# The first steps of a fused attention, ReLU-squared MLP and top-1 MoE kernel in another order

## The chip, the cores and the metric

One core of one Trainium2 chip. The metric is the device time of one execution in microseconds; lower is better.

## The reference

Inputs: q, k, v of 4 x 8 x 768 x 64, 8 memory keys and values per head, w_in 512 x 2048, w_out 2048 x 512, eight experts' w1 (512 x 1024) and w2 (1024 x 512), and two gates of 512 x 8. What is computed, cut down:

```python
for c in range(24):                      # chunks of 32 queries, 56 keys of context and 8 memory keys
    scores = scale * q_c @ concat(mem_k, k_ctx).T
    a = exp(scores - max(scores)); a /= sum(a) + 1e-9
    out[c] = a @ concat(mem_v, v_ctx)
x = out as 3072 x 512                    # tokens x (heads x 64)
r = maximum(x @ w_in, 0); x = (r * r) @ w_out
e = argmax(x @ w_gate); p = softmax(x @ w_gate)[e]; s = sigmoid((x @ w_output_gate)[e])
out = p * s * (maximum(x @ w1[e], 0) @ w2[e])
```

## The kernel before

Tokens are cut into 24 units of 128 (u), 12 pairs of units (`Duo`, d0 to d11) and, for the MLP, 12 blocks of 256 (`Block`, b0 to b11; block n is pair n). All products are 3-pass: each operand is split into a rounded part (hi) and the rest (lo), and hi x hi, lo x hi and hi x lo are added.

A pair goes through `scores_mm` (TensorE, L161), `scores_max` and `scores_sub` (VectorE, L190 and L195), `scores_exp` (ScalarE, L211), `norm` (VectorE, L217 to L221), `transpose_a_mm` and `transpose_a_copy` (TensorE L234, ScalarE L244), `av_mm` (TensorE, L161, or L259 in the later form), `av_scale` (VectorE, L274), `transpose_x_mm`, `transpose_x_hi` and `transpose_x_lo` (TensorE L234, ScalarE L299, VectorE L303). Each of these takes one unit or both.

w_in and w_out are cut into eight tiles each, i0 to i7 and o0 to o7, of 1 MB; `tiles` numbers them i0, o0, i1, o1 and so on, so number 13 is o6 and number 15 is o7. Each is loaded (`load_w`) and split in six steps: `split_w_exp` (ScalarE's Abs, L327), `split_w_shift` (VectorE, L332), `split_w_or` in two steps (VectorE, L339 and L343), `split_w_hi` (ScalarE's cast, L352) and `split_w_lo` (VectorE's long difference, L357). Raw tiles share three buffers, and the converted ones two.

A block takes, for each of 16 slices f, `mm1_products` (L410; L389 for two blocks at once), `relu` (ScalarE L421, L429 and L433, then VectorE's short difference L435) and `mm2` (L446 to L448). Weight tile n serves the slices 2n and 2n + 1. After the MLP come the gates, pairs of tiles sorted by expert, and the rest by slots; the change doesn't touch them.

The order on each engine is the order of the program text. The opening is written out by hand, from `keep_busy(12)` to the loop over `seq`; `keep_busy(n)` (L1010 to L1012) issues n products of a tile of ones that nobody reads. `hold` (L996) makes a load wait, by letting GpSimd copy one number into the tile that the load is to fill. The transfers of the opening go out on one queue, SP's: two inputs of 128 x 1248 float32 for d0 (0.64 MB each), an identity (0.07 MB), d0's v (1.05 MB), half of i0 (0.52 MB), and behind the first hold the other half, d1's inputs, o0 and d1's v. From the fifth slice on, `plan(n, fn)` puts a step behind place n of `seq`, and within a place `turn` sorts the steps: hi and shift first, then lo, loads and pairs' steps, or, and Abs last. `bits` holds the place of each weight tile's or-step.

## Time and profile before

| what | us |
|---|---|
| median of 3 runs | 962.99 (961.12 to 965.63) |
| the profiled execution | 961.27 |
| its span, first to last instruction | 959.4 |
| TensorE busy | 944.5 |
| VectorE busy | 600.1 |
| ScalarE busy | 453.0 |
| GpSimd busy | 95.1 |

The trace is of the one profiled execution. Its times run from the start of the span. Engines are named PE (TensorE's products), PEld (its weight loads), DVE (VectorE), ACT (ScalarE), POOL (GpSimd) and SP. Two steps of one engine can overlap by some 0.08 us in the rows where the second doesn't need the first.

### The profile page before, as it was taken

The numbers are of one execution on the slowest core, as the hardware profiler recorded it, in microseconds if no ns is written. First come the engines' busy times: TensorE is split into PE (matmuls) and PEld (weight loads), VectorE is DVE, ScalarE is ACT, GpSimd is POOL, SyncE is SP. The second block draws the span as 40 slices with busy tenths as digits, with TensorE's granted clock in tenths as the row PEclk, the third lists the DMA queues.
The fourth block names the chain that finished last, engine by engine and source line by source line (L and its number), as shares of the span: only waits on it lengthen the run. The fifth ranks groups of instructions, "written<-read, shape, count | busy, mean of one in ns | idle before, by whom it ended". The sixth has DMA issues, their size and how long they took to land. (4 is left out here: it accounts for less than half of the span.)

```text
span 959.4 us, 19441 instructions
## 1 busy us (share of the span) xinstructions
PE 944.5 (98%) x7862; PEld 791.2 (82%) x7862; DVE 600.1 (63%) x1125; ACT 453.0 (47%) x816; POOL 95.1 (10%) x93
## 2 busy tenths in 40 slices
PE   8999999999999999999999999999999999999996
PEld 5787798888888888888888888889999999888885
DVE  6999663554445444534553454658776666799995
ACT  4687533333333233322322333545444555688885
POOL 0000000000000000000000011012222211212221
PEclk9999999999999999999999999999999999999999
DMA  9466512214020212021100106360886656443631
GB/s 358 174 219 235 170 68 99 77 24 119 24 77 24 85 58 77 24 76 59 48 1 1 45 1 247 126 241 25 333 316 237 235 206 245 187 175 132 219 124 42
DMA packets 30991, 125.51 MB, mean 131 GB/s; under 512 B 8559, under 2 KB 9071, under 8 KB 21554
## 3 DMA queue, kind: packets, MB, share of 16 engines
q1 hardware_dynamic: 25650, 110.30, 32.0%
q0 software_dynamic: 5248, 13.92, 4.0%
q8 instruction: 64, 1.05, 0.5%
q14 instruction: 29, 0.24, 0.1%
HBM read 138.65 MB, written 13.61 MB: 159 GB/s over the span
## 5 line engine op out<-in xcount | busy, mean ns | idle before, releaser
L389 PE MATMUL ph<-xhi,wi 128*128 128x512 f32 x688 | 212.7, 390 | 0.3 <-DVE wi L357 0.3
L421 ACT ACTIVATE r<-ph 128x256 f32<-128x256 f32 x192 | 72.2, 376 | 233.2 <-PE ph L389 199.1
L431 DVE TENSOR_TENSOR g<-r 128x256 f32<-128x256 f32 x160 | 67.6, 423 | 183.1 <-ACT r L421 183.0
L446 PE MATMUL py<-wo,gh 128*128 128x512 f32 x384 | 156.1, 407 | 0.8 <-ACT gh L433 0.8
L389 PEld LDWEIGHTS ph<-xhi,wi 128*128 128x128 f32 x688 | 129.1, 188 | 28.4 <-DVE wi L357 1.2
L447 PE MATMUL py<-wo,gh 128*128 128x512 f32 x384 | 150.1, 391 | 0.0
L448 PE MATMUL py<-wo,gl 128*128 128x512 f32 x384 | 150.0, 391 | 0.0
L389 PE MATMUL ph<-xlo,wi 128*128 128x512 f32 x344 | 133.9, 389 | 0.0
L686 DVE TENSOR_TENSOR x<-raw,x 128x1024 fp32r<-128x1024 f32 x88 | 103.2, 1223 | 7.0 <-ACT x L685 5.4
L435 DVE TENSOR_TENSOR gl<-g,gh 128x256 fp32r<-128x256 f32 x192 | 81.6, 425 | 29.1 <-ACT gh L433 7.3
L686 DVE TENSOR_TENSOR p<-raw,p 128x1024 fp32r<-128x1024 f32 x64 | 78.2, 1222 | 22.1 <-ACT p L685 21.0
L685 ACT CAST x<-raw 128x1024 fp32r<-128x1024 f32 x88 | 87.4, 1056 | 0.0
L446 PEld LDWEIGHTS py<-wo,gh 128*128 128x128 f32 x384 | 72.1, 188 | 17.4 <-issue 2.0
L448 PEld LDWEIGHTS py<-wo,gl 128*128 128x128 f32 x384 | 72.1, 188 | 16.1 <-DVE gl L435 0.6
L433 ACT ACTIVATE gh<-r 128x256 fp32r<-128x256 f32 x192 | 80.1, 417 | 10.6 <-PE py L447 2.3
L447 PEld LDWEIGHTS py<-wo,gh 128*128 128x128 f32 x384 | 72.3, 188 | 12.4
L543 POOL DMA_INDIRECT listd<-ent,idx x24 | 24.7, 1030 | 551.6 <-DVE idx L541 339.0
L389 PEld LDWEIGHTS ph<-xlo,wi 128*128 128x128 f32 x344 | 64.6, 188 | 13.5
L685 ACT CAST p<-raw 128x1024 fp32r<-128x1024 f32 x64 | 66.6, 1041 | 0.6 <-DMA raw<-in_wexp 0.6
L835 PE MATMUL po<-x,ht 128*128 128x512 f32 x264 | 65.5, 397 | 0.7 <-DVE ht L825 0.7
L835 PEld LDWEIGHTS po<-x,ht 128*128 128x128 f32 x264 | 48.1, 188 | 10.3 <-DVE ht L825 1.1
L705 POOL DMA_INDIRECT out<-o,slots x27 | 35.2, 1304 | 210.4 <-ACT o L701 91.4
(229 smaller groups left out, 1453.1 us busy)
## 6 DMA issues: line engine op xcount, KB each, us to landing
raw<-in_wexp SPq DMA_DIRECT2D x82, 1024.0 KB
kv<-in_kv SPq DMA_DIRECT2D x19, 880.0 KB
raw_o<-in_w_out SPq DMA_DIRECT2D x8, 1024.0 KB
raw_i<-in_w_in SPq DMA_DIRECT2D x7, 1024.0 KB
ydram<-y SPq DMA_DIRECT2D x24, 256.0 KB
q<-in_qt SPq DMA_DIRECT2D x20, 256.0 KB
qk<-in_qk SPq DMA_DIRECT2D x4, 624.0 KB
v<-in_vv SPq DMA_DIRECT2D x2, 1024.0 KB
```

Of the source, the lines that this page charges most:

```text
L389: nc.tensor.matmul(ph.rearrange("p (s c) -> p s c", s=2), lhsT=w_in_part(w, f, k), rhs=x[:, s, k, :], start=(n == 0), stop=(n == 11),)
L421: nc.scalar.activation(self.r, self.ph, ACTF.Relu, scale=WSCALE)
L431: nc.vector.tensor_tensor(g, r, r, op=ALU.mult)
L433: nc.scalar.activation(gh, r, ACTF.Square)
L435: nc.vector.tensor_tensor(gl, g, gh.bitcast(F32), op=ALU.subtract)
L446: nc.tensor.matmul(self.y[t], lhsT=gh[:, s], rhs=w_out_part(wh, f), start=(f == 0), stop=False)
L447: nc.tensor.matmul(self.y[t], lhsT=gh[:, s], rhs=w_out_part(wl, f), start=False, stop=False)
L448: nc.tensor.matmul(self.y[t], lhsT=gl[:, s], rhs=w_out_part(wh, f), start=False, stop=(f == NF - 1))
L685: nc.scalar.copy(w[:, 0], t)
L686: nc.vector.tensor_tensor(w[:, 1], t, w[:, 0].bitcast(F32), op=ALU.subtract)
L705: nc.gpsimd.indirect_dma_start(out=out, out_offset=bass.IndirectOffsetOnAxis(ap=slots[:, c, 0:1].bitcast(U32), axis=0), in_=self.y[t], in_ ...
L835: nc.tensor.matmul(self.po, lhsT=self.ht[:, part, f, :], rhs=w[:, wp, j * D : j * D + D], start=(f == 0 and part == 0 and wp == 0), stop=( ...
```

## The change

It does four things. It takes 16 of the 42 dummy products out and orders the steps of the first pair anew: both units' maxima come before the first hold's loads, `norm` of unit 1 goes ahead, and the second hold (on i1) waits for i0's first half instead of for unit 1's sums. It makes d1's scores by unit, unit 1 in another bank of PSUM. It puts the split of i1 and o1 in another order. And in the plan the Abs of tile 13 (o6) goes one place later, and the cast and the long difference of tile 15 (o7) go to pair 2's places.

```diff
@@ -887,12 +887,16 @@
     bits = dict(zip(range(3, 16), (2, 4, 6, 8, 10, 12, 14, 15, 17, 18, 20, 21, 26)))
     for m, n in bits.items():
         if m > 4:
-            plan(bits[m - 1], split_w_exp, *tiles[m])
-            plan(bits[m - 1] + 1, split_w_shift, *tiles[m])
+            if m == 13:
+                plan(bits[m - 1] + 1, lambda x=tiles[m]: (split_w_exp(*x), split_w_shift(*x)))
+            else:
+                plan(bits[m - 1], split_w_exp, *tiles[m])
+                plan(bits[m - 1] + 1, split_w_shift, *tiles[m])
         if m > 3:
             plan(n, split_w_or, *tiles[m])
-            plan(n + 1, split_w_hi, *tiles[m])
-            plan(n + 1, split_w_lo, *tiles[m])
+            if m < 15:
+                plan(n + 1, split_w_hi, *tiles[m])
+                plan(n + 1, split_w_lo, *tiles[m])
         if m > 6:
             plan(bits[m - 3] + 1, load_w, *tiles[m])
     plan(16, duos[2].load_q, 0)
@@ -905,6 +909,8 @@
     plan(23, lambda: prepare())
     n = at[2, 0]
     plan_duo(2, n - 7, n - 7, n - 4, n - 3)
+    plan(n - 4, lambda: split_w_hi(*tiles[15]))
+    plan(n - 3, split_w_lo, *tiles[15])
     plan_duo(3, n + 1, n + 2, n + 5, n + 6)
     plan_gate(0, n + 7, n + 9, n + 15, n + 18)
     plan_duo(4, n + 11, n + 13, n + 15, n + 17)
@@ -1012,48 +1018,45 @@
                 nc.tensor.matmul(spin, lhsT=ones, rhs=ones.unsqueeze(1).to_broadcast([P, 4, P]), start=True, stop=True)
 
         u0, u1, other = (0,), (1,), (ps_y, "y")
-        keep_busy(12)
+        keep_busy(8)
         d0.scores_mm(u0)
-        keep_busy(4)
         d0.scores_max(u0)
+        d0.scores_sub(u0)
+        d0.scores_mm(u1, *other)
+        d0.scores_exp(u0)
+        d0.scores_max(u1)
         i0t = load_w(*i0, issue=False)
-        hold(i0t[:, 1024:].bitcast(F32), d0.mx[u0][0:1, 0, 0:1])
+        hold(i0t[:, 1024:].bitcast(F32), d0.mx[u1][0:1, 0, 0:1])
         load_w(*i0, halves=b)
         d1.load_first_qk(0)
         d1.load_first_qk(1)
         load_w(*o0)
         d1.load_first_v()
-        d0.scores_sub(u0)
-        d0.scores_mm(u1, *other)
-        d0.scores_exp(u0)
+        d0.scores_sub(u1)
         d0.transpose_a_mm(u0)
         d0.transpose_a_copy(u0)
-        keep_busy(3)
-        d0.scores_max(u1)
-        d0.scores_sub(u1)
+        keep_busy(2)
         d0.scores_exp(u1)
-        split_w_exp(*i0, a)
         d0.norm(u0)
         d0.av_mm(u0)
+        d0.norm(u1)
+        split_w_exp(*i0, a)
         d0.av_scale(u0)
+        d0.transpose_a_mm(u1, *other)
+        d0.transpose_a_copy(u1)
         split_w_shift(*i0, a)
         split_w_or(*i0, a, steps=(0,))
-        d0.transpose_a_mm(u1, *other)
-        d0.transpose_a_copy(u1)
         d0.transpose_x_mm(u0)
         d0.transpose_x_hi(u0)
+        d0.av_mm(u1, *other)
         split_w_exp(*i0, b)
-        keep_busy(2)
-        d0.av_mm(u1, *other)
         d0.transpose_x_lo(u0)
-        d0.norm(u1)
+        d0.av_scale(u1)
+        split_w_or(*i0, a, steps=(1,))
         i1t = load_w(*i1, issue=False)
-        hold(i1t.bitcast(F32), d0.r[u1][0:1, 0, 0:1])
+        hold(i1t.bitcast(F32), converted[i0][0:1, 0:1])
         load_w(*i1)
         nc.sync.dma_start(cst[:, P:], consts[:, P:])
-        d0.av_scale(u1)
-        keep_busy(5)
-        split_w_or(*i0, a, steps=(1,))
         d0.transpose_x_mm(u1, *other)
         split_w_shift(*i0, b)
         split_w_hi(*i0, a)
@@ -1061,20 +1064,24 @@
         split_w_or(*i0, b, steps=(0,))
         split_w_lo(*i0, a)
         d0.transpose_x_lo(u1)
+        d1.scores_mm(u0)
         split_w_or(*i0, b, steps=(1,))
-        d1.scores_mm()
+        split_w_hi(*i0, b)
+        d1.scores_max(u0)
+        d1.scores_sub(u0)
+        d1.scores_mm(u1, *other)
+        d1.scores_exp(u0)
+        split_w_lo(*i0, b)
         keep_busy(2)
         b0.mm1_products(0)
-        split_w_hi(*i0, b)
         load_w(*o1)
-        d1.scores_max()
-        split_w_lo(*i0, b)
+        d1.scores_max(u1)
         split_w_exp(*o0)
         keep_busy(3)
-        d1.scores_sub()
+        d1.scores_sub(u1)
         b0.relu(0)
         b0.mm1_products(1)
-        d1.scores_exp()
+        d1.scores_exp(u1)
         split_w_shift(*o0)
         split_w_or(*o0, steps=(0,))
         keep_busy(3)
@@ -1094,20 +1101,22 @@
         d1.transpose_x_mm()
         split_w_shift(*i1)
         d1.transpose_x_hi()
+        split_w_or(*i1, steps=(0,))
         b0.mm2(0)
         d1.transpose_x_lo()
         split_w_exp(*o1)
         b0.mm2(1)
-        split_w_or(*i1)
+        split_w_or(*i1, steps=(1,))
+        split_w_hi(*i1)
         load_w(*o2)
         b1.mm1_products(0)
         split_w_shift(*o1)
+        split_w_or(*o1, steps=(0,))
+        split_w_lo(*i1)
         b1.relu(0)
-        split_w_hi(*i1)
         b1.mm1_products(1)
-        split_w_lo(*i1)
         b1.mm2(0)
-        split_w_or(*o1)
+        split_w_or(*o1, steps=(1,))
         b1.relu(1)
         split_w_exp(*i2)
         split_w_hi(*o1)
```

At the place of o6, ScalarE's order before (`raw_o_1008` is o6, `wo_1059` is o5, `wi_1083` is i6, `r`, `g` and `gh` are relu steps of the slices 9 and 10):

```order
L352 CAST wo_1059<-ws_o_975 128x1024
L327 ACTIVATE ws_o_1067<-raw_o_1008 128x1024
L421 ACTIVATE r_9_1075<-ph_9_1038 128x256
L429 ACTIVATE g_9_1077<-r_9_1075 128x256
L433 ACTIVATE gh_9_1079<-r_9_1075 128x256
L352 CAST wi_1083<-ws_i_1030 128x1024
L421 ACTIVATE r_10_1108<-ph_10_1095 128x256
L429 ACTIVATE g_10_1110<-r_10_1108 128x256
L433 ACTIVATE gh_10_1112<-r_10_1108 128x256
```

and now, where o6 is `raw_o_997` and i6 is `wi_1070`:

```order
L352 CAST wo_1048<-ws_o_964 128x1024
L421 ACTIVATE r_9_1062<-ph_9_1027 128x256
L429 ACTIVATE g_9_1064<-r_9_1062 128x256
L433 ACTIVATE gh_9_1066<-r_9_1062 128x256
L352 CAST wi_1070<-ws_i_1019 128x1024
L327 ACTIVATE ws_o_1073<-raw_o_997 128x1024
L421 ACTIVATE r_10_1097<-ph_10_1084 128x256
L429 ACTIVATE g_10_1099<-r_10_1097 128x256
```

The Abs of o6 (L327) has gone from in front of slice 9's second relu to behind the cast of i6 and in front of slice 10's relu.

At the place of o7, ScalarE's order before (`wo_1369` is o7; L244 copies pair 2's transposed scores, the steps around it are slices 13 and 14):

```order
L433 ACTIVATE gh_13_1365<-r_13_1361 128x256
L352 CAST wo_1369<-ws_o_1142 128x1024
L421 ACTIVATE r_14_1393<-ph_14_1380 128x256
L429 ACTIVATE g_14_1395<-r_14_1393 128x256
L433 ACTIVATE gh_14_1397<-r_14_1393 128x256
L244 COPY e_1312<-psa_0_1401 128x1024
L421 ACTIVATE r_14_1417<-ph_14_1380 128x256
```

and now, where o7 is `wo_1397`:

```order
L433 ACTIVATE gh_13_1354<-r_13_1350 128x256
L421 ACTIVATE r_14_1379<-ph_14_1366 128x256
L429 ACTIVATE g_14_1381<-r_14_1379 128x256
L433 ACTIVATE gh_14_1383<-r_14_1379 128x256
L244 COPY e_1301<-psa_0_1387 128x1024
L352 CAST wo_1397<-ws_o_1131 128x1024
L421 ACTIVATE r_14_1405<-ph_14_1366 128x256
```

The cast (L352) stood three steps ahead of the copy and now stands right behind it.

Where i1 and o1 are split, VectorE's order before (`wi` is i1, `ws_o` is o1, `gl` the short differences of block 1's first two slices):

```order
L357 TENSOR_TENSOR wo_574<-ws_o_444,wo_574 128x1024
L332 TENSOR_SCALAR ws_i_572<-ws_i_572 128x1024
L303 TENSOR_TENSOR xlo<-pst_0_583,xhi 128x2x4x128
L339 SCALAR_TENSOR_TENSOR ws_i_572<-raw_i_334,ws_i_572 128x1024
L343 SCALAR_TENSOR_TENSOR ws_i_572<-raw_i_334,ws_i_572 128x1024
L332 TENSOR_SCALAR ws_o_602<-ws_o_602 128x1024
L435 TENSOR_TENSOR gl_0_634<-g_0_630,gh_0_632 128x256
L357 TENSOR_TENSOR wi_636<-ws_i_572,wi_636 128x1024
L339 SCALAR_TENSOR_TENSOR ws_o_602<-raw_o_439,ws_o_602 128x1024
L343 SCALAR_TENSOR_TENSOR ws_o_602<-raw_o_439,ws_o_602 128x1024
L435 TENSOR_TENSOR gl_1_667<-g_1_663,gh_1_665 128x256
```

and now:

```order
L357 TENSOR_TENSOR wo_563<-ws_o_434,wo_563 128x1024
L332 TENSOR_SCALAR ws_i_561<-ws_i_561 128x1024
L339 SCALAR_TENSOR_TENSOR ws_i_561<-raw_i_325,ws_i_561 128x1024
L303 TENSOR_TENSOR xlo<-pst_0_572,xhi 128x2x4x128
L343 SCALAR_TENSOR_TENSOR ws_i_561<-raw_i_325,ws_i_561 128x1024
L332 TENSOR_SCALAR ws_o_592<-ws_o_592 128x1024
L339 SCALAR_TENSOR_TENSOR ws_o_592<-raw_o_430,ws_o_592 128x1024
L357 TENSOR_TENSOR wi_601<-ws_i_561,wi_601 128x1024
L435 TENSOR_TENSOR gl_0_627<-g_0_623,gh_0_625 128x256
L343 SCALAR_TENSOR_TENSOR ws_o_592<-raw_o_430,ws_o_592 128x1024
L435 TENSOR_TENSOR gl_1_656<-g_1_652,gh_1_654 128x256
```

The first or-step of i1 (L339) has gone ahead of the step on x (L303), and block 1's first short difference (L435) behind o1's first or-step and i1's long difference.

## Rows read from the trace of the kernel before

**Rows 1.** Stretches: busy us of PE, PEld, DVE, ACT, POOL, then granted clock, DMA share, GB/s.

```profile
40.00:100.00 60.00, 59.20 (x379) 47.76 (x378) 56.21 (x71) 47.53 (x89) 0.00 (x0) 1.00 0.63 224
100.00:130.00 30.00, 27.85 (x383) 23.75 (x382) 17.93 (x26) 11.75 (x26) 0.00 (x0) 1.00 0.34 118
```

**Rows 2.** Waits of TensorE, whole span: us in total, times, longest.

```profile
PE psx L259 <- ACT e L244: 2.1, 1, 2.1
PE py L446 <- ACT gh L433: 0.8, 1, 0.8
```

**Rows 3.** Timeline, 107 to 117 us: start, us, engine, line, operation, count, idle before.

```profile
107.79 0.39 PE L389 MATMUL ph<-xlo,wi 128*128 128x512 f32 x1
...
109.56 1.05 ACT L352 CAST wo<-ws_o 128x1024 fp32r<-128x1024 f32 x1 [3.72 <-DVE ws_o L343]
...
110.52 0.37 ACT L421 ACTIVATE r<-ph 128x256 f32<-128x256 f32 x1
...
111.55 0.99 ACT L244 COPY e<-psa 128x1024 f32<-128x1024 f32 x1
...
112.60 0.25 PE L259 MATMUL psx<-e,v 64*64 64x32 f32 x2 [2.15 <-ACT e L244]
...
116.10 0.63 PE L389 MATMUL ph<-xhi,wi 128*128 128x512 f32 x2
```

**Rows 4.** Timeline, 83 to 87 us, ScalarE, TensorE and VectorE.

```profile
83.23 1.16 ACT L327 ACTIVATE ws_o<-raw_o 128x1024 f32<-128x1024 f32 x1 [1.29 <-DVE wo L357]
...
85.47 0.50 PE L446 MATMUL py<-wo,gh 128*128 128x512 f32 x1 [0.80 <-ACT gh L433]
...
85.52 0.42 DVE L435 TENSOR_TENSOR gl<-g,gh 128x256 fp32r<-128x256 f32 x1
...
85.63 1.06 ACT L352 CAST wi<-ws_i 128x1024 fp32r<-128x1024 f32 x1 [0.21 <-DVE ws_i L343]
...
85.85 0.69 DVE L332 TENSOR_SCALAR ws_o<-ws_o 128x1024 int32<-128x1024 int32 x1
...
86.59 0.38 ACT L421 ACTIVATE r<-ph 128x256 f32<-128x256 f32 x1
```

**Rows 5.** Timeline of TensorE, 1 to 8 us.

```profile
1.01 4.97 PE L1012 MATMUL spin<-ones 128*128 128x512 bf16 x12 [1.01 <-POOL ones L990]
5.92 0.86 PE L161 MATMUL pss<-qk 64*32 64x64 f32 x64
6.71 1.04 PE L1012 MATMUL spin<-ones 128*128 128x512 bf16 x4
```

**Rows 6.** Stretches of the opening.

```profile
0.00:4.00 4.00, 2.98 (x8) 1.04 (x9) 0.00 (x0) 1.28 (x1) 0.41 (x5) 1.00 0.54 195
4.00:8.00 4.00, 4.00 (x108) 1.90 (x106) 1.15 (x2) 0.00 (x0) 0.18 (x1) 1.00 1.00 375
6.00:30.00 24.00, 20.74 (x596) 14.14 (x597) 21.77 (x36) 13.07 (x21) 1.89 (x8) 1.00 0.88 342
```

**Rows 7.** Timeline, 19 to 23 us, VectorE and ScalarE.

```profile
19.44 1.22 DVE L190 TENSOR_REDUCE mx<-pss 128x16 f32<-128x1024 f32 x1
...
20.09 1.16 ACT L327 ACTIVATE ws_o<-raw_o 128x1024 f32<-128x1024 f32 x1
...
21.15 0.37 ACT L421 ACTIVATE r<-ph 128x256 f32<-128x256 f32 x1
...
22.31 0.43 DVE L435 TENSOR_TENSOR gl<-g,gh 128x256 fp32r<-128x256 f32 x1
```

**Rows 8.** Timeline, 31 to 39 us, VectorE and TensorE.

```profile
31.50 1.23 DVE L303 TENSOR_TENSOR xlo<-pst,xhi 128x1024 fp32r<-128x1024 f32 x1 [0.97 <-ACT xhi L299]
...
35.79 0.43 DVE L435 TENSOR_TENSOR gl<-g,gh 128x256 fp32r<-128x256 f32 x1
...
37.30 0.39 PE L389 MATMUL ph<-xhi,wi 128*128 128x512 f32 x1
38.02 0.50 PE L389 MATMUL ph<-xhi,wi 128*128 128x512 f32 x1 [0.33 <-DVE wi L357]
```

## Prediction

> **What bounds the kernel now.** I read the stretches first, then TensorE's waits, then the timelines at the places of the edits. By stretch TensorE is busy 59.20 of the 60 us from 40 to 100, and 27.85 of the 30 to 130 us [rows 1]. Busy time of a pipelined engine is not work at its peak, but it says where TensorE waits at all, and the list of its waits names the two largest that lie behind the opening: 2.1 us for a copy on ScalarE and 0.8 for a square on ScalarE [rows 2]. So the time is TensorE's products, plus the opening, plus a few waits while weights are still being split. In that stretch VectorE is the near rival: 56.21 of 60 us [rows 1]. What the change can win or lose lies in these waits, some microseconds of 961, against 4.8 us for 0.5%, which is about what a measurement of this kernel can tell from no change.
>
> **Term 1: the cast of o7 goes behind the copy.** Before, ScalarE sits 3.72 us until VectorE has or-ed o7, casts it at 109.56 (1.05 us), runs three small steps and at 111.55 copies the transposed scores of pair 2 (0.99); TensorE waits 2.15 us for that copy, to 112.60 [rows 3]. The relu behind the cast needs only the products that end with the one begun at 107.79 (0.39 us), so without the cast in front it starts at 108.2. From relu to copy it takes 111.55 - 110.52 = 1.03, so the copy runs from 109.2 to 110.2, and TensorE, which was free at 112.60 - 2.15 = 110.45, need not wait. That is worth 2.15 us at most, or a little more where its last product's tail counts, and 0 at least, if the wait only moves on; I take -2.2, since every row of this chain is there. Does the cast come too late now? It runs from 110.2 to 111.3; behind it come the other block's three small steps (1.1) and on VectorE a short difference (0.43), then o7's long one (1.23): done near 114. TensorE needs o7 only after the step that begins at 116.10 in this trace [rows 3], 3.5 us behind the end of the wait: now 110.45 + 3.5 = 113.95, and twelve products of 0.63 - 0.39 = 0.24 later 116.8. That leaves 2.8 us of cover.
>
> **Term 2: one weights' step later (o6).** Before, ScalarE's Abs of o6 stood in a hole: it waited 1.29 us for its buffer and ran from 83.23 to 84.39; TensorE waited 0.80, to 85.47, for the square queued behind it [rows 4]. Now relu and squares go first, which ends that wait. But TensorE's third product there needs VectorE's short difference, which stands behind the same or-steps as before and ended only near 85.9, so nothing is won. And the Abs (1.16) now stands behind the cast at 85.63, in front of the relu at 86.59 [rows 4]: that relu and what hangs on it come 1.0 us later, and VectorE's shift of o6 (85.85) goes behind i6's long difference and waits for the Abs. VectorE has no room here (56.21 of 60 us), so it stays 1.0 behind, and TensorE waits that much longer over the next steps. I take +1.0; the ends are 0 (TensorE had slack after all) and 1.2 (the whole Abs).
>
> **Term 3: the opening.** Sixteen of the 42 dummy products go: 4 + 4 + 1 + 2 + 5. The first twelve take 4.97 us from 1.01 [rows 5], some 0.43 each for 512 columns: the lower of TensorE's two clock levels (1.2 GHz), though the column of the granted clock prints 1.00 there [rows 6]. The next four take 1.04, the higher level [rows 5]. With eight, the first scores can start at 1.01 + 8 x 0.43 = 4.4 instead of 5.92, if their input is there: 0.64 MB, first in the queue, which moved 195 GB/s x 4 us = 0.78 MB by 4.0 [rows 6]. At the low level they take up to twice the 0.79 of 5.92 to 6.71, so VectorE's first maximum starts by 6.0, which is 0.8 early.
>
> From there I added VectorE's and ScalarE's durations in the new order. Pair 1's first maximum comes at 17.8 instead of 19.44 [rows 7]: 1.6 early, 0.8 from the start and the rest from waits that the new order fills. But ScalarE's exponential of unit 0 (0.63) now stands ahead of the Abs of o0, and needs maximum and subtraction first: 17.8 + 0.73 + 0.72 = 19.25, then 0.6, so the Abs starts at 19.85 instead of 20.09, the relu at 20.9 instead of 21.15, and VectorE's difference at 22.1 instead of 22.31 [rows 7]. Of 1.6 us 0.2 is left; VectorE stands 1 us for that difference, and TensorE 2 us for the relu.
>
> From there the order is the same until i1 is split. The 0.97 us that VectorE waited before 31.50 is now filled with an or-step [rows 8], which is a gain; yet i1's long difference and an or-step of o1 now stand ahead of block 1's first short difference (35.79 before). By the durations that comes at 36.85. On ScalarE the cast of i1 also stands ahead of that block's relu, so its products start at 36.2 instead of 35.85, the third waits to 37.3, and the next step starts at 38.25. Before, that step started at 37.30 and its second product waited 0.33, to 38.02 [rows 8], which is a start at 37.8 without the wait. So the wait for i1 is gone, and a longer one for block 1's difference stands in its place. I take **+0.4**. Bounds: -1.6 if the lead is kept, +1.0 if the 0.2 is lost too and the waits come full.
>
> The first hold now waits for unit 1's maximum, so the second half of i0 is issued 0.7 to 0.9 us later. 2.92 MB stand ahead of it, of which (195 + 375) x 4 = 2.28 MB have moved at 8.0 [rows 6]; the rest lasts to 9.7. I cost it at nothing; if that cover is short, everything behind it in the queue lands up to 0.9 late, within the bounds. The hold on i1 ends about when it did.
>
> **Sum.** -2.2 + 1.0 + 0.4 = -0.8 us. The profiled execution took 961.27 us (its span 959.4 and 1.87 around it), so 960.5; the median of the runs shown is 1.72 above that execution, so **962.2 us** as a median.
>
> **A rule that speaks against it.** In the trace TensorE's wait of 2.15 us is its largest [rows 3], and the stretch around it still has the granted clock at 1.00 [rows 1], the higher level: a gap of that size did not cost the clock. The Trainium skill (TensorE: Matmul & The Clock Gate, Why this matters for your kernels) says to keep TensorE busy without a break to reach the high clock, and to leave no long idle gaps between bursts, because throughput drops after them; by that rule an opening with fewer dummies would run slower, as rival C does. The new opening's largest gap, about 2 us near 20, is of the size that the row shows harmless; that many gaps close together are harmless no row here shows.
>
> **Rivals.** A, the lead is kept: if the Abs of o0 is not what decides, the opening gives its 1.6, and -2.2 + 1.0 - 1.6 = -2.8: 960.2. Against it stands ScalarE's single queue. Chance 0.12.
>
> B, the cast's move wins nothing, because TensorE waits for the next thing instead (the transposed x, or o7's difference): +1.0 + 0.4 = +1.4: 964.4. For it: VectorE is nearly full until 100 us. Against it: the 2.8 us of cover. Chance 0.18.
>
> C, slower: the clock. TensorE stays at, or falls back to, the low level until its dense stretch at 30 us. It is busy 20.74 us from 6 to 30 us [rows 6], of which 30 dummies of 1.04 / 4 = 0.26 are 7.8 [rows 5]; the other 12.9 take as much again at half the clock. VectorE is busy 21.77 of these 24 us, and its work hides about half: +6.5 on the forecast, 968.7. It decides only if the low level lasts to about 25 us; to 14 us it would cost 1 to 1.5, which is inside the range. Chance 0.05.
>
> The forecast's mechanism has 0.62, and 961.0 to 963.6 is its own range. The last 0.03 is for a gain over 4.8 us, for which I see no row.
>
> **Chances.** The forecast, A and B all lie within 0.5% of 962.99 (958.2 to 967.8): 0.92. Slower is C, 0.05; faster 0.03. The range for 8 in 10 takes A and B in, and the spread of the runs themselves (961.12 to 965.63): 959.2 to 965.4.
>
> **What would show it.** In the profile after: TensorE's 2.1 us wait for the copy is gone, and o7's cast stands behind the copy; TensorE waits for VectorE's short difference around 86, 92 or 96 us, in all about 1 us longer than it waited there before; the first scores start near 4.4 us, pair 1's first maximum near 17.8, block 0's first short difference still near 22; no wait for i1 at 38, but some 0.7 us for block 1's difference at 37. Dummies about 0.25 us apart near 9 us show the high clock; 0.43 apart there, or later, would show C. The prediction is wrong if TensorE's work behind 113 us stands more than 2.5 us from where these terms put it, 0.8 us early.

## The result, and the profile after

| what | before | after |
|---|---|---|
| median, us | 962.99 (961.12 to 965.76, 5 runs) | 970.98 (970.04 to 971.11, 5 runs) |
| ratio, with its 95% interval | | 1.0075 [1.0054, 1.0096] |
| the profiled execution, us | 961.27 | 970.04 |
| its span, us | 959.4 | 967.7 |

The change makes the kernel 8.0 us slower, 0.8%, against a forecast of 0.8 us faster. Three places lose what the forecast did not have, and one wins what it had. The stretches come first (length, busy time and number of instructions of each engine; then the granted clock, the DMA share and GB/s).

```profile
16.00:24.00 8.00, 7.37 (x150) 5.92 (x151) 5.57 (x11) 3.88 (x8) 0.00 (x0) 0.57 1.01 419
...
100.00:130.00 30.00, 30.00 (x511) 25.65 (x492) 18.91 (x29) 14.10 (x34) 0.00 (x0) 1.00 0.43 149
...
204.00:212.00 8.00, 5.42 (x36) 4.25 (x36) 2.56 (x3) 1.06 (x1) 0.00 (x0) 0.57 0.32 50
212.00:220.00 8.00, 8.00 (x38) 6.56 (x37) 5.53 (x15) 1.71 (x5) 0.00 (x0) 1.00 0.01 3
```

From 100 to 130 us TensorE is busy all 30 us, where it was 27.85 [rows 1]: the wait is gone. But in two stretches of 8 us the granted clock is 0.57: the lower of its two levels, 1.2 GHz, for most of the stretch (half clock, below). In the profile of before TensorE runs at that level only in the first 5.5 us and in the last 1.5.

The list of TensorE's waits (engine, tile, line, releaser: us in total, times, longest) has lost the 2.1 us for ScalarE's copy [rows 2], and has a new first entry:

```profile
PE pss L161 <- issue: 4.3, 1, 4.3
```

"Issue" means that TensorE stood 4.3 us for nothing that the profile shows. The timeline tells where (start, us, operation, count, and in brackets the idle time ahead with its releaser):

```profile
201.00 1.31 PE L161 MATMUL pss<-kv,q 64*32 64x64 f32 x105
206.59 0.68 PE L161 MATMUL pss<-kv,q 64*32 64x64 f32 x23 [4.28 <-issue]
...
207.78 0.63 PE L447 MATMUL py<-wo,gh 128*128 128x512 f32 x1
208.21 0.63 PE L448 MATMUL py<-wo,gl 128*128 128x512 f32 x1
```

These small products are pair 5's scores, 128 of them. In the kernel before they ran in one piece:

```profile
200.36 1.51 PE L161 MATMUL pss<-kv,q 64*32 64x64 f32 x128
...
202.13 0.40 PE L447 MATMUL py<-wo,gh 128*128 128x512 f32 x1
202.37 0.39 PE L448 MATMUL py<-wo,gl 128*128 128x512 f32 x1
...
204.65 0.62 PE L389 MATMUL ph<-xhi,wi 128*128 128x512 f32 x2
```

Now TensorE stands 4.28 us behind the 105th, and then products that came 0.23 us apart come 0.43 apart, to 211.2: 4.6 us of work at half clock, which loses 2.3. The product that began at 204.65 begins here at 211.89:

```profile
211.89 0.62 PE L389 MATMUL ph<-xhi,wi 128*128 128x512 f32 x2
```

Ahead of the burst the changed kernel was 201.00 - 200.36 = 0.64 us late, behind it 211.89 - 204.65 = 7.24. So **6.6 of the 8.3 us between the spans (967.7 - 959.4) are lost at one place that the change never touches**.

What is there? TensorE's own instructions arrive by DMA, on a queue of their own (packets, MB, share of 16 engines). Over the whole execution:

```profile
q8 instruction: 63, 1.03, 0.5%
```

In the transfers of the stretch from 202.6 to 205.5 us alone:

```profile
q8 instruction: 1, 0.02, 5.9%
```

And of the stretch from 187 to 190 us, which holds the packet ahead of that one:

```profile
q8 instruction: 1, 0.02, 2.4%
```

63 packets carry 1.03 MB, which is 16 KB each; the trace has 7846 products and 7967 weight loads of TensorE, so a packet holds some 250 instructions, or about 125 products with their loads. That the queue is TensorE's is read from this number alone: the other engines' instructions are far too few for it. One of these packets lies in TensorE's stand and takes 5.9% of 16 engines x 2.9 us = 2.7 us; the one ahead took 2.4% of 16 x 3 = 1.2.

Another 1.1 us are lost far behind pair 5's scores, at 694 us, among the experts' products, where the kernel before has no wait (from the list of TensorE's waits):

```profile
PE ph2p L735 <- DVE gl2p L746: 1.0, 1, 1.0
```

On VectorE that difference stands behind the split of a tile of an expert's weights. ScalarE's cast of that tile waited for its load until 688.11, 8.3 us later than the same cast before (679.80), where TensorE was 7.3 us late. Of the later runs e3 and e9 have this wait too (0.54 and 0.78 us), e5 and e12 don't; no run takes it apart, and its cause stays open.

The third loss is in the opening. TensorE's timeline there:

```profile
15.98 0.93 PE L161 MATMUL pss<-qk 64*32 64x64 f32 x64 [0.94 <-DMA qk<-in_qk]
17.54 1.33 PE L161 MATMUL pss<-qk 64*32 64x64 f32 x64 [0.63 <-DMA qk<-in_qk]
...
20.06 0.42 PE L410 MATMUL ph<-xlo,wi 128*128 128x256 f32 x1
...
23.72 0.28 PE L410 MATMUL ph<-xlo,wi 128*128 128x256 f32 x1
```

d1's scores wait 0.94 and 0.63 us for their q and k, and behind them block 0's first products are 0.42 us long at half clock; those from 23.72 on are 0.28. VectorE's first short difference (22.31 before [rows 7]) shows what that costs:

```profile
17.91 0.68 DVE L190 TENSOR_REDUCE mx<-pss 128x8 f32<-128x512 f32 x1
...
23.61 0.43 DVE L435 TENSOR_TENSOR gl<-g,gh 128x256 fp32r<-128x256 f32 x1 [2.36 <-ACT gh L433]
```

Ahead of it on ScalarE stand the Abs of o0 and the relu, and the relu waits for those products:

```profile
19.95 1.14 ACT L327 ACTIVATE ws_o<-raw_o 128x1024 f32<-128x1024 f32 x1
22.44 0.38 ACT L421 ACTIVATE r<-ph 128x256 f32<-128x256 f32 x1 [1.35 <-PE ph L410]
```

And the part that won. ScalarE's copy now stands ahead of the cast, as the prediction had it [rows 3], and TensorE waits for neither:

```profile
111.87 0.40 ACT L433 ACTIVATE gh<-r 128x256 fp32r<-128x256 f32 x1
112.18 0.99 ACT L244 COPY e<-psa 128x1024 f32<-128x1024 f32 x1
113.07 1.04 ACT L352 CAST wo<-ws_o 128x1024 fp32r<-128x1024 f32 x1
```

What the two edits of the plan did is read from three places of TensorE's timeline: the last product ahead of the wait of 0.80 us [rows 4], pair 2's first scores, and pair 5's above. Before:

```profile
84.29 0.39 PE L448 MATMUL py<-wo,gl 128*128 128x512 f32 x1
...
96.93 0.86 PE L161 MATMUL pss<-k,q 64*32 64x64 f32 x64
```

And after:

```profile
86.20 0.39 PE L448 MATMUL py<-wo,gl 128*128 128x512 f32 x1
...
87.91 0.50 PE L448 MATMUL py<-wo,gl 128*128 128x512 f32 x1 [0.86 <-DVE gl L435]
...
99.79 0.86 PE L161 MATMUL pss<-k,q 64*32 64x64 f32 x64
```

The changed kernel is 1.91 us late at the first, 2.86 at the second and 0.64 at the third.

### The profile page after: what moved, and what is told of

Same layout as the page of the kernel before. It is cut to its first block, busy times and chain, and to the rows that moved or that the text cites. A ratio compares the mean times of both kernels' runs of the same rounds, so it can differ in the third digit from the quotient of the medians.

```text
span 967.7 us, 19412 instructions
## 1 busy us (share of the span) xinstructions
PE 946.0 (98%) x7846; PEld 794.5 (82%) x7846; DVE 600.1 (62%) x1127; ACT 452.3 (47%) x817; POOL 97.4 (10%) x93
## 3 DMA queue, kind: packets, MB, share of 16 engines
q8 instruction: 63, 1.03, 0.5%
## 5 line engine op out<-in xcount | busy, mean ns | idle before, releaser
L421 ACT ACTIVATE r<-ph 128x256 f32<-128x256 f32 x192 | 72.2, 376 | 239.9 <-PE ph L389 205.5
L435 DVE TENSOR_TENSOR gl<-g,gh 128x256 fp32r<-128x256 f32 x192 | 81.5, 425 | 34.0 <-ACT gh L433 12.4
```

The lines of the kernel that those rows point to most:

```text
L421: nc.scalar.activation(self.r, self.ph, ACTF.Relu, scale=WSCALE)
L435: nc.vector.tensor_tensor(gl, g, gh.bitcast(F32), op=ALU.subtract)
```

## The experiments

**Theory 1**: the change takes 16 products with their weight loads out of TensorE's program. That moves the places where its 16 KB packets begin and end, and one of them now keeps TensorE waiting inside a burst of short products, which also costs the clock. **Rival 2**: the loss is the activity of the missing dummies. **Rival 3**: the new order or the plan carries it. In the expectations the burst near 201 us is called pair 6's until the twelfth run; counted from 0 it is pair 5's.

### The count of TensorE's instructions alone: e1_dummies_back, e2_short_dummies, e3_before_shifted

The 16 dummies back into the changed kernel:

```diff
-        keep_busy(8)
+        keep_busy(12)
...
+        keep_busy(4)
         d0.scores_mm(u1, *other)
...
-        keep_busy(2)
+        keep_busy(3)
         d0.scores_exp(u1)
...
+        keep_busy(2)
         d0.av_mm(u1, *other)
...
+        keep_busy(5)
         d0.transpose_x_mm(u1, *other)
```

> The changed kernel with all 16 dummy products put back (12 at the start, then 4, 3, 2 and 5 at about their old places); the new order, the scores by unit and the plan stay. Nobody reads the dummies, so the output is unchanged. Theory 1 (instruction count: 32 instructions fewer on TensorE move the 16 KB instruction fetches, and one of them now falls into pair 6's burst of short products near 202 us): the 4.3 us stand at 202 us and the 6.8 us at half the clock behind it are gone, about 7.7 us less, and the half-clock stretch at 16.6 to 23.4 us goes too: 961 to 963.5. Rival 2 (the dummies' activity in the opening carries the whole loss): 961 to 963.5 as well, but then the stand at 202 us is still there. Rival 3 (the new order or the plan carries it): unchanged, 970 to 971.

The changed kernel with the same dummy columns, in more and shorter products (`keep_busy_short(n, k)` issues n products of 128 k columns):

```diff
-        keep_busy(8)
+        keep_busy_short(16, 1)
+        keep_busy_short(8, 2)
```

> The changed kernel with its first eight dummies of 512 columns cut into 24 (16 of 128 columns, 8 of 256): the same 4096 columns, but 16 products more in the program, so the fetches of TensorE's instructions fall where they fell in the kernel before. Theory 1 (instruction count): no stand at 202 us and full clock from there on, while the half-clock stretch near 16 to 23 us stays; 970.98 - 7.7 = 963.3. Rival 2 (activity of the missing dummies): 971. Rival 3 (order or plan): 971.

And the kernel before with 112 products more:

```diff
-        keep_busy(12)
+        keep_busy_tiny(118)
+        keep_busy(6)
```

> The kernel before with 6 of its first 12 dummies replaced by 118 tiny ones (1 x 4 outputs): 112 products more, about the same time, and since a fetch holds 128 products with their weight loads, the fetches fall where they fall in the changed kernel; order and plan are those of before. Theory 1 (instruction count): a stand of some 4 us in pair 6's burst near 201 us, half clock for some 7 us behind it, 962.99 + 7.7 = 970.7. Rivals 2 and 3: 963 to 964.5 (the opening may lose up to 1.5 if the tiny products leave the clock low for longer).

Measured: 961.43 us (ratio to before 0.999 [0.9976, 1.0005]), **961.86** (0.9984 [0.9969, 0.9999]), and **971.84** (1.0095 [1.0069, 1.0120]). TensorE's timeline of the burst with the short dummies:

```profile
200.97 1.62 PE L161 MATMUL pss<-kv,q 64*32 64x64 f32 x128
```

And with the kernel before and 112 products more:

```profile
207.29 1.26 PE L161 MATMUL pss<-kv,q 64*32 64x64 f32 x101
210.69 0.56 PE L161 MATMUL pss<-kv,q 64*32 64x64 f32 x3 [2.14 <-issue]
212.62 0.81 PE L161 MATMUL pss<-kv,q 64*32 64x64 f32 x24 [1.37 <-issue]
```

The second run settles it for the large loss. It leaves the order, the plan and the dummies' columns as the change has them, and even its opening has the half clock (0.57 from 16 to 24 us); its burst starts at 200.97, against 201.00, so it is as late as in the changed kernel. Yet with 16 products more the burst runs in one piece, and 9.1 us are gone (8.2 between the profiled spans, 959.5 and 967.7). The third is the mirror: the order and plan of before, and a stand of 2.14 + 1.37 us behind products 101 and 104, with half clock behind it. 112 more and 16 fewer give nearly the same place, as they must if a packet holds 128 products with their loads (e10 below bears that out). Its excess isn't all from there: it also stands 1.70 us in d1's scores, loses the clock in the opening (21.3 to 24.7 us) and at 117 us (below), and its profiled execution (974.87) is among its slower ones. Rivals 2 and 3 fall for the large loss.

### The terms one by one: cast_only, step_only

Term 1 alone in the kernel before, and term 2 alone:

```diff
-            plan(n + 1, split_w_hi, *tiles[m])
-            plan(n + 1, split_w_lo, *tiles[m])
+            if m < 15:
+                plan(n + 1, split_w_hi, *tiles[m])
+                plan(n + 1, split_w_lo, *tiles[m])
...
+    plan(n - 4, lambda: split_w_hi(*tiles[15]))
+    plan(n - 3, split_w_lo, *tiles[15])
```

> The kernel before with one edit: the cast and the long difference of o7 go to pair 2's places. Term 1 of the prediction: the 2.15 us wait for the copy is gone, TensorE's work behind 113 us stands 2.2 us earlier, 960.8. Rival B: another wait takes its place, 963.0. Theory 1 on instruction fetches: TensorE's count is that of before, so no stand at 202 us in either case.

```diff
-            plan(bits[m - 1], split_w_exp, *tiles[m])
-            plan(bits[m - 1] + 1, split_w_shift, *tiles[m])
+            if m == 13:
+                plan(bits[m - 1] + 1, lambda x=tiles[m]: (split_w_exp(*x), split_w_shift(*x)))
+            else:
+                plan(bits[m - 1], split_w_exp, *tiles[m])
+                plan(bits[m - 1] + 1, split_w_shift, *tiles[m])
```

> The kernel before with one edit: the Abs of o6 goes one place later. Term 2 of the prediction: TensorE stands 1.0 us longer between 86 and 100 us, so 1.0 us more, 964.0 against 963. Its lower end: 0. TensorE's 2.1 us wait for the copy near 113 us is still there. A further question to its profile: of 28 executions of the kernel before, 12 lie at 960.1 to 961.5 us with a mean granted clock of 0.998 to 1.0 and 16 at 962.9 to 965.6 with 0.993 to 0.997. If that wait sometimes costs the clock, this kernel's times fall into two such groups too, and a profile of the upper one shows half clock just behind 113 us; if the groups come from somewhere else, half clock stands elsewhere.

The cast alone: **959.12 us, ratio 0.9959 [0.9943, 0.9975]**, the fastest version of this study. In its profile the wait is gone; pair 2's scores start 0.4 us later than before (97.32 against 96.93, an opening that varies by as much between executions), and pair 5's 1.83 earlier (198.53 against 200.36): 2.2 us, the forecast. But the median fell by 4.2 (963.31 to 959.12 in that comparison), twice that. The profile of the other run, 963.61 us (1.0008 [0.9995, 1.0022]), tells why. There the wait is still in place, and what follows it is (TensorE's timeline):

```profile
113.83 0.25 PE L259 MATMUL psx<-e,v 64*64 64x32 f32 x2 [2.10 <-ACT e L244]
...
117.17 0.63 PE L447 MATMUL py<-wo,gh 128*128 128x512 f32 x1
117.60 0.63 PE L448 MATMUL py<-wo,gl 128*128 128x512 f32 x1
...
118.38 0.39 PE L447 MATMUL py<-wo,gh 128*128 128x512 f32 x1
```

And two stretches behind it (columns as above):

```profile
114.90:118.20 3.30, 3.30 (x74) 2.95 (x67) 0.83 (x2) 1.01 (x1) 0.00 (x0) 0.50 0.22 32
118.20:122.00 3.80, 3.80 (x18) 3.13 (x17) 0.77 (x1) 0.20 (x1) 0.00 (x0) 0.99 0.56 214
```

One microsecond behind the 2.10 us wait the clock is at half for 3.4 us, which costs 1.5: TensorE is 113.83 - 112.60 = 1.23 us behind the kernel before at the first of these products and 118.38 - 115.64 = 2.74 at the last. In the profile of e3_before_shifted a wait of 2.13 us at the same place is followed by 6.8 us at 0.50 (116.8 to 123.6 us). In the profile of before a wait of 2.15 cost nothing [rows 1, 3]. So the same wait costs the clock in some executions only. That fits the times: of the 28 executions of before beside cast_only, 12 lie at 960.1 to 961.5 us with a mean granted clock of 0.998 to 1.0, and 16 at 962.9 to 965.6 with 0.993 to 0.997, while all nine of cast_only lie at 958.6 to 960.3. Of step_only's ten, two lie at 961.9 and 962.0 with 0.998 and eight, the profiled one among them, at 963.1 to 964.6 with 0.996 to 0.997. Against the lower group alone (middle 961.1) the moved cast wins 2.0 us, about the wait itself. That the upper group of before lost its clock at just this wait is inferred: no profile of before fell into it.

The Abs one place later gives TensorE the waits that the prediction named: 0.86 us for a short difference at 86, 0.28 at 92 and 0.28 at 96, in place of the 0.80 of [rows 4], so 0.6 more. In time it is 0.9 more: step_only is 84.62 - 84.29 = 0.33 us late ahead of these waits and 98.19 - 96.93 = 1.26 behind them. A wait costs more than its bracket says, since what the product ahead of it still had to run is taken off; before, 84.29 to 85.47 is 0.95 more than the usual 0.23, for a wait of 0.80. The medians can't tell 0.9 us (0.9995 to 1.0022).

### The opening: e7_early_hold, e8_best, e13_hold_cast, e14_hold_cast_12

e7 is the version with short dummies and this edit (the loads behind the hold move up with it):

```diff
         d0.scores_max(u0)
+        i0t = load_w(*i0, issue=False)
+        hold(i0t[:, 1024:].bitcast(F32), d0.mx[u0][0:1, 0, 0:1])
+        load_w(*i0, halves=b)
...
         d0.scores_sub(u0)
...
-        hold(i0t[:, 1024:].bitcast(F32), d0.mx[u1][0:1, 0, 0:1])
```

> The changed kernel with its first eight dummies cut into 24 shorter ones of the same columns (so no stand at 202 us), and the first hold back on unit 0's maximum, as before. If the late hold is what makes pair 1's q and k land late (TensorE waits 0.94 and 0.63 us for them before the two halves of d1's scores): those waits go, d1's scores end 1 to 1.5 us earlier, and the half-clock stretch near 17 to 23 us may go with them; TensorE's work at 200 us stands 0.5 to 1.5 us earlier than with the short dummies alone: 960.5 to 961.4 against 961.9. If the hold is covered, as the prediction had it: no difference, 961.9.

e8 is e1 with the same early hold, and the Abs of o6 at its old place.

> What the terms point to: the changed kernel with all 16 dummies back, the first hold on unit 0's maximum, the cast of o7 moved as in the change, and the Abs of o6 left where it was. By the terms: the cast moved alone gave 959.1; the Abs of o6 at its old place saves 1.0 against the version with the dummies back (961.4): 960.4, and the early hold 0 to 1 more: 959.4 to 960.4. If the new order of the opening wins anything of its own, it comes out under 959.1.

e13 is the changed kernel with the early hold, the Abs at its old place, and dummies cut behind d1's scores; e14 adds four dummies at the start.

```diff
-        keep_busy(5)
+        keep_busy_short(20)
```

> The changed kernel with the first hold on unit 0's maximum, the Abs of o6 at its old place, and the five dummies behind the first pair of d1's transposes cut into 20 short ones of nearly the same columns, so that 15 products more lie between the opening's bursts and pair 5's. The fetch boundary in d1's scores then falls behind product 68, as in the changed kernel, where TensorE changes units, and the one in pair 5's burst where it falls in the kernel before. Theory 1: no stand at 201 us, little or none in d1's scores; the late hold's 1.6 us are won: below 959.1, by the terms 957.5 to 959. If the missing dummies cost the clock by themselves, half clock in the opening and 960 or more.

```diff
-        keep_busy(8)
+        keep_busy(12)
...
-        keep_busy(5)
+        keep_busy_short(16)
+        keep_busy(1)
```

> As the last one, with 12 dummies at the start as in the kernel before, and 12 products more (four dummies cut into 16) behind d1's scores: the boundary in d1's scores falls behind product 64, between its units. It tells whether the four first dummies matter by themselves: if the clock is granted later without them, this one is faster, 957 to 958.5; if they only take time (the first scores start at 6 instead of 4.5 us), it is up to 1.5 us slower than the last one, 959 to 960.

| version | first hold | dummies | half clock behind the first 8 us | first step of two blocks | median |
|---|---|---|---|---|---|
| before | early | all | none | 37.8 | 962.99 |
| changed kernel | late | 26 | 16.6 to 23.4 | 40.16 | 970.98 |
| e1 | late | all | none | 39.63 | 961.43 |
| e2 | late | 26, eight of them cut | 16.7 to 23.5 | 40.23 | 961.86 |
| e7 | early | 26, eight of them cut | none | 38.65 | 961.50 |
| e8 | early | all | none | 39.47 | 960.51 |
| e13 | early | 26, five of them cut | 16.6 to 23.5 | 41.12 | 961.31 |
| e14 | early | 30, four of them cut | 15.2 to 22.0 | 40.01 | 961.03 |

Three things follow.

With all dummies the clock holds in the opening. With fewer it falls in every profile but e7's, with either hold (in e5, e9 and e12 below, too). And e7's profile is not a usual one of e7: it has a mean granted clock of 0.998, the other nine executions 0.992 to 0.997. e14, which has the first twelve back, falls too, while e8 with the same order and all of them doesn't, so by these profiles it is those between the steps that keep it up.

What the early hold is worth isn't shown. From e2 to e7 the first step starts 1.6 us sooner, but e7's profile also kept the clock, and the medians differ by 0.4. From e1 to e8 it is 0.2, with a stand for a packet of 2.30 instead of 0.82 us. In e13 the early hold lets the loads of pair 1's q and k go out at 7.09, in e12 the late one at 8.44 (8.15 before, 8.61 in the changed kernel); still, e13's second half of d1's scores waits for them until 16.41, and e12's goes on at 15.99.

And no version of the new opening reaches that of before: e8 was to come out at 959.4 to 960.4 and took 960.51, e13 was to beat 959.1 and took 961.31, e14 was to take 960 at most and took 961.03; none beats the moved cast alone.

What holds them up is again a packet. d1's scores are 128 small products, and in the kernel before TensorE stands 0.56 us behind the 52nd. Its timeline there:

```profile
16.65 0.76 PE L161 MATMUL pss<-qk 64*32 64x64 f32 x52
17.96 1.00 PE L161 MATMUL pss<-qk 64*32 64x64 f32 x76 [0.56 <-issue]
```

In e8 it is 2.30:

```profile
15.63 0.76 PE L161 MATMUL pss<-qk 64*32 64x64 f32 x52
18.69 1.02 PE L161 MATMUL pss<-qk 64*32 64x64 f32 x76 [2.30 <-issue]
```

### The place of the packets in the opening: e10_best_shifted, e11_cast_shifted

e8 and cast_only with 57 products more, in the same way (`keep_busy_short` of n alone: 128 columns):

```diff
-        keep_busy(12)
+        keep_busy_short(48)
...
-        keep_busy(4)
+        keep_busy_short(16)
...
-        keep_busy(3)
+        keep_busy_short(12)
```

> The version with the dummies back, the early hold, the cast moved and the Abs of o6 at its old place (960.5), with its dummies of 512 columns at the first three places cut into four each: 57 products more at the same columns, so every fetch boundary falls 57 products earlier in the program. There, 2.30 us of standing lay within d1's scores, behind product 52 of 128, where a boundary falls. Theory 1: that stand is gone or under 0.8 us, and what is won is up to 2: 958.5 to 959.5; a new stand at another place would show where the boundary went. If the stand there has another cause: 2.3 us again and 960.5.

> The kernel before with the cast and the long difference of o7 moved (959.1), and 57 products more in the same way (the dummies of 512 columns at the first three places cut into four each). Its stand behind product 52 of d1's scores took 0.82 us. Theory 1: that stand is gone, 958.3 to 958.8, unless the boundary now falls into another burst, there or later, and costs the same or more. If the stand has another cause: unchanged, 959.1.

Both got worse: 966.75 us (1.0058 [1.0040, 1.0077]) and 966.50 (1.0036 [1.0010, 1.0061]). The stand isn't gone; there are three now, in e10's timeline of TensorE:

```profile
12.12 0.97 PE L161 MATMUL psx<-v,spare_o 64*32 64x64 f32 x50 [1.31 <-issue]
...
18.59 0.38 PE L1015 MATMUL spin<-ones 128*128 128x512 bf16 x1 [1.04 <-issue]
...
19.33 1.47 PE L161 MATMUL pss<-qk 64*32 64x64 f32 x122
23.60 0.31 PE L161 MATMUL pss<-qk 64*32 64x64 f32 x6 [2.81 <-issue]
```

The last is behind product 122 of d1's scores (123 in e11), where 52 - 57 + 128 = 123 was to be expected; with 16 products fewer it lies behind product 67 (e5, e9, e12, e13; 52 + 16 = 68 expected), with 112 more behind 68. With 12 fewer (e14) TensorE waits 0.98 us between the units, at 64, as expected, but the profile puts that wait down to the scores themselves. The changed kernel has no stand at 67: it waits for q and k at 64. So the place follows the count to within one product, over four counts. What it costs there doesn't: 0.56 to 0.92 us with the opening and count of before, 0.8 to 2.3 with the new opening, 2.81 and 4.66 in these two. Around these stands both lose the clock, though they have all the dummies' columns: e10 from 12.2 to 15.6 us, e11 from 22.5 to 29.3. The expectation that a place outside d1's burst costs nothing was wrong, since the next place is only 128 products on.

### Why that packet is late: e5_q_later, e9_q_after_burst, e12_q_after_burst5

The q loads of the next pair go out in the same moment. First they were planned three places later, which moved nothing (they wait for a buffer that the burst frees, and SP issued the first at 202.32, against 201.89 in the changed kernel), and then behind the maxima of the wrong pair:

```diff
-            plan(s + 1, duos[b + 1].load_q, 0)
-            plan(s + 1, duos[b + 1].load_q, 1)
+            plan(s + 4, duos[b + 1].load_q, 0)
+            plan(s + 4, duos[b + 1].load_q, 1)
```

> The changed kernel, instruction count as it is, with one edit: the two q loads that each pair issues for the next one go from one place behind its scores to four places behind. Theory 1a (the fetch is slow near 202 us because the q loads go out in the same moment: their 2 KB packets lie beside a fetch that takes 2.75 us, where most others take about 1): the fetch in pair 6's burst takes about 1 us, the stand at 202 us falls from 4.3 to 2 us or less, and the clock may hold: 963 to 968. Theory 1b (the fetch is slow there whatever is beside it): stand and time unchanged, 970 to 971.

```diff
+            if until is not None:
+                nc.gpsimd.tensor_copy(self.q[t][0:1, 0, 0:1], until.mx[BOTH][0:1, 0, 0:1])
...
+            for t in range(TPB):
+                plan(s + 1, duos[b + 1].load_q, t, d if b == 6 else None)
```

> The changed kernel with one edit: the two q loads of pair 7, which wait for a buffer that pair 6's burst itself frees, now also wait (through a copy on GpSimd) for that pair's maxima, so they go out behind the whole burst. The instruction count of TensorE is that of the changed kernel. Theory 1a (the q packets beside it make that fetch slow): the fetch near 202.7 us takes about 1 us instead of 2.75, and since TensorE went on 1.1 us behind the fetch's end, the stand falls from 4.3 to about 2.5 us; with half clock for 3.4 to 6.8 us behind it 967 to 969.5. Theory 1b (it is slow by itself): 2.7 us again, stand 4.3, 970 to 971.

These two are repeats of the changed kernel as far as 201 us goes: 967.68 and 968.40 us, stands of 0.28 + 2.59 and 3.35 us. The third has `b == 5`:

> The changed kernel with one edit, now at the right place (the burst near 201 us is pair 5's, counted from 0; the run before this one put its copy behind pair 6's, at 258 us): the two q loads of pair 6, which wait for a buffer that pair 5's burst itself frees, also wait through a copy on GpSimd for that pair's maxima, so they go out behind the whole burst. TensorE's instruction count is that of the changed kernel. Theory 1a (the q packets beside it make that fetch slow): the fetch near 203 us takes about 1 us instead of 2.75, the stand falls from 4.3 to about 2.5 us, 967 to 969.5. Theory 1b (slow by itself): 2.3 to 2.8 us again, stand 3.3 to 4.3, 968.4 to 971.

TensorE's timeline of the burst (L161 is L163 in this run):

```profile
200.19 1.20 PE L163 MATMUL pss<-kv,q 64*32 64x64 f32 x99
201.95 0.45 PE L163 MATMUL pss<-kv,q 64*32 64x64 f32 x3 [0.56 <-issue]
204.26 0.75 PE L163 MATMUL pss<-kv,q 64*32 64x64 f32 x26 [1.86 <-issue]
```

And the transfers from 201.5 to 205.5 us:

```profile
DMA packets 1, 0.02 MB, mean 4 GB/s; under 512 B 0, under 2 KB 0, under 8 KB 0
...
q8 instruction: 1, 0.02, 4.9%
```

The q loads now go out at 206.55, and the instruction packet is the only one in these 4 us. It still takes 4.9% of 16 x 4 = 3.1 us. So the q loads don't make it slow, and theory 1a falls, although the stand is 0.56 + 1.86 = 2.4 us, as 1a had it. The time, 966.22 (1.0041 [1.0023, 1.0059]), lies below what either theory gave; the stands of the four programs with this count differ anyway (4.28 us in the changed kernel, 2.87, 3.35 and 2.42 in e5, e9 and e12), so one profile of e12 doesn't show that the edit shortened it. What makes this packet take three times as long as others, in this kernel as in before (where nothing waits for it), stays open; so does why a program of 16 products more doesn't wait in this burst at all.

## Why the prediction was wrong

Forecast 962.2 us, with 959.2 to 965.4 as the range; measured 970.98, outside it and on the other side of no change.

**Term 1, the cast (-2.2 forecast): right.** Between pair 2's scores (99.79, against 96.93) and pair 5's (201.00, against 200.36) the changed kernel makes up 2.2 us, and cast_only 2.2. Nothing took the wait's place; the cover of 2.8 us for o7's difference held. Rival B, that the move wins nothing, is out.

**Term 2, o6's Abs (+1.0): right.** TensorE waits 0.86, 0.23 and 0.30 us for the named steps, and between 84.29 and pair 2's scores the changed kernel falls back from 1.91 to 2.86 us, which is 0.95; step_only falls back 0.93.

**Term 3, the opening (+0.4): wrong.** It cost 2.4 at the first step of two blocks (40.16 instead of 37.8) and 1.9 at 84.29. The chain on VectorE and ScalarE came as worked out: the first scores at 4.54 (4.4 forecast), pair 1's first maximum at 17.91 (17.8), the Abs of o0 at 19.95 (19.85). Then the relu, forecast for 20.9, started at 22.44, because it waited 1.35 us for TensorE: the products ran at half clock, as shown above. At full clock the 3.4 us from 18.80 to 22.20 would be 1.7 (an estimate), and the products would be done before the Abs is.

The step that failed is the one that set rival C aside: that the gaps of the new opening, the largest about 2 us, are of a size that does no harm. That largest gap never came. The clock fell at 16.6, ahead of it, behind gaps of 0.81, 1.21 and 0.94 us; from 8.0 to 16.6 TensorE was busy 5.25 us, against 6.88 before. The prediction had itself left open that many gaps close together are harmless. The profile of e7, which has the early hold, dummies of as many columns as the changed kernel's, and the clock kept, is 84.68 - 84.29 = 0.39 us late at that product: the forecast's +0.4. "I cost it at nothing", on the later first hold, is not shown to be wrong: the loads of q and k went out 0.46 us later than before (8.61 and 8.15). TensorE waits for them 0.94 + 0.63 us because it gets there at 15.04, where before it came at 16.65; the working for VectorE and ScalarE didn't ask when they land. At full clock that wait would have stayed hidden, by the estimate above.

**The sum.** -2.2 + 1.0 + 1.9 = +0.7 against -0.8, and 0.64 was measured at pair 5's scores. This part of the miss is 1.4 us, inside the range's width.

**What the sum had no term for**: 6.6 us at pair 5's scores, the stand for an instruction packet and the clock behind it. The prediction counted a dummy as time on TensorE; it is also 2 instructions of a program that is fetched in pieces, and e2 and e3 show that the number of products alone makes the stand come and go. The 1.1 us at 694 us had no term either.

**Rival C, the clock**, had 0.05 and 968.7 us. The number is near and the mechanism half right: the opening did fall to half clock, from 16.6 to 23.4 us, but that is 0.5 us (the first step against e1's, whose first scores start 1.7 us later) to 1.5 (against e7's) of the loss; that its number came near is luck. The Trainium skill (TensorE: Matmul & The Clock Gate, Why this matters for your kernels) warns of idle gaps between bursts of products, since throughput drops behind them. step_only's trace has such a drop behind a wait of 2.10 us, which is shorter than the gaps that the Trainium skill names there. The prediction had set one row against a drop, the wait of 2.15 us that cost nothing. One execution's row didn't show that a gap is safe, only that it had been so once.

## What to carry to other kernels

A product taken out of a tuned program, or put in, moves every later place where the engine waits for its next instructions; look at the bursts of short instructions behind the edit, and count instructions as well as time. When a time moves at a place that the edit doesn't touch and the engine stands there for "issue", cut a harmless instruction in two until the old count is back, with the work equal: that one run tells the program's length from everything else. And a wait of some 2 us on TensorE may cost as much again in clock in some executions, so take it out for its own size and count the rest as a chance; here the moved cast alone won 4 us in the median where its row showed 2.2.

## What the runs showed of the hardware that was not expected

TensorE's instructions come in packets of 16 KB while the kernel runs, 63 or 64 of them (q8's 1.03 MB in the changed kernel), and TensorE can stand for one: up to 4.7 us. In the openings it went on 1.3 to 1.4 us behind the end of the packet (in that of before the packet ends at 15.72 + 0.97 = 16.69, and TensorE goes on at 17.96). In pair 5's burst there is no such rule: 1.1 us behind it in the changed kernel (202.72 + 2.74 = 205.46, on at 206.59), 0.4 to 1.0 in e5, e9 and e3, and ahead of the packet's end in e12, which the runs don't explain. That TensorE waits for the packet is read from these times and from the count that moves the stand; no run could take a packet away.

Half clock set in during a stand in pair 5's burst, or up to 1.7 us behind it, in all five programs that stood there for 2.4 us or more in all (the changed kernel, e3, e5, e9, e12), and in none of the others; e11 stood there for 0.18.
